# Attention parts dealt by their columns over one unit less, and a job's values one item later

## The chip, the core and the metric

The kernel runs on one core of a Trainium2 chip. The metric is the device time of one execution in microseconds. Three runs of the kernel before took 695.48, 698.78 and 702.34 us; the median is 698.78.

## The reference

Attention over 2 batches, 8 heads, 576 positions and heads of 64, with a bias from a running sum, feeds a two-layer block with an exponential unit, and that feeds four experts whose outputs are added with weights by token.

```python
scores = scale * np.matmul(q, k.transpose(0, 1, 3, 2))
cum = np.cumsum(np.maximum(s, 0.0), axis=-1)
bias = -(cum[:, :, :, None] - cum[:, :, None, :])
scores = np.where(causal, -1e9, scores + np.minimum(bias, 0.0))
attn = np.exp(scores - np.max(scores, axis=-1, keepdims=True))
attn = attn / (np.sum(attn, axis=-1, keepdims=True) + 1e-09)
x = np.matmul(attn, v)                        # then as 1152 rows of 512
h = x @ w_in                                  # 512 -> 2048
x = np.where(h > 0, h, np.exp(np.minimum(h, 0)) - 1) @ w_out
p = domain_probs / (domain_probs.sum(-1, keepdims=True) + 1e-09)
for e in range(4):                            # 512 -> 1024 -> 512
    out += p[:, e:e + 1] * (np.maximum(x @ w1[e], 0.0) @ w2[e])
```

## The kernel before

The 1152 tokens are worked in groups (`GROUPS`): a first group of 256 tokens, and the other 896 as two halves of 448 (`N2`). The attention of the first group is written out by hand at the start (`attention_first`). Then the first group goes through the first layer (`layer1`, 16 units of 128 hidden columns) and the experts (32 units), and the attention of all later tokens is threaded between these matmuls. Last, both layers are done for the 896 tokens (`both`), with the products of a Strassen scheme; this end is outside the change.

One unit is one call of `slot`: the up matmuls of a unit (12 of 256 columns in the experts, tile `up`), its activation (ScalarE and VectorE, tile `gt`), the preparation of a later unit's weights (ScalarE rounds them, VectorE takes the rest, tile `wu`), and the down matmuls of the unit some places back (6 of 512 columns, tiles `acc`). Units are numbered from 0; 16 is the end of the first layer, and 50 the end of the first group. Three times in a unit, at a third, at two thirds and at its end, `slot` calls `background`, and that hands out waiting work.

The waiting work is first the list of `attention_parts`. A job is one pair of heads of one batch and a range of queries (`JOBS`): 4 small jobs of 128 queries, then 4 of 320 and 4 of 448. Its items are blocks of 128 queries of one head (or 64 of both). Each item gives score parts (`scores`: matmuls L554, L556, L562, L563, on VectorE the bias and the maximum at L596, on ScalarE the exponential at L603), and three items later (`LATE`) transpose parts (`transposes`: VectorE's scaling L576 by `normalise`, TensorE L613, ScalarE's copy L625 or L628 into tile `pt`). After the transposes of a job's last item come its values (`values`: TensorE L640 reads `pt` and `v`; ScalarE copies the result into tile `xa` at L643), and behind them the loads of the job after next on SyncE's queue. The first score part of an item also prepares q and k of the next one where a new head begins (`split`: L539 to L542 on ScalarE, L90 on VectorE, two small loads at L536). Scores, transposes and values take their PSUM bank in turn from four (`ps_att`).

`Background` deals the list by count: at unit position `at` it has done the share of its parts that a line through (14, 0), (18, 0.06) and (45, 1) gives (`BG_FROM`, `BG_EVEN`, `BG_SLOW`, `BG_TO`). After 45 a second list is dealt out until 50 (`early_parts`): the splits of the later tokens' first blocks (tile `x2a`) and the sums and splits of the first two weight pairs of the end (tiles `sums`, `top`, `w`).

This order is what is written down; a scheduler then orders each engine's instructions by what it takes to be ready, so matmuls of one part can stand among those of another.

Of the kernel before, what the change touches and what calls it, by code (L numbers as in the profile page):

```python
# [37 lines left out]
LAG = 2  # L38
LATE = 3

BG_FROM, BG_EVEN, BG_TO = 14, 18, 45
BG_SLOW = 0.06

DEC = 4
# [8 lines left out]
def tile_kernel(ctx, tc, qT, kT, v, s, w64, w, probs, out):  # L53
# [20 lines left out]
    def sb(shape, tag, bufs, dtype=F32):  # L74
        p = (base if tag in BASE else edge if tag in EDGE else l1_pool if tag in L1
             else held if tag == "wr"
             else att_pool[0])
        return p.tile(shape, dtype, tag=tag, name=tag, bufs=bufs)
# [6 lines left out]
    def ps_att():  # L85
        n_att[0] += 1
        return ps(*(("att", 2), *spare)[n_att[0] % (1 + len(spare))])
# [363 lines left out]
    def attention_parts(x):  # L451


        items, jobs, small = [], [], []
        for b, chunks, col in JOBS:
            cb = CHUNKS[b]
            q0, q1 = cb[chunks[0]], cb[chunks[-1] + 1]
            for hp in range(HP):
                job = dict(b=b, chunks=chunks, col=col, q0=q0, q1=q1, hp=hp)
# [109 lines left out]
        def normalise(every=False):  # L569
            if not norm or len(norm) < 2 and not every:  # L570
                return
            sm = totals.pop()[:, :len(norm)]
            DVE.tensor_scalar(sm, sm, 1e-9, None, op0=ALU.add)
            DVE.reciprocal(sm, sm)
            for i, p in enumerate(norm):
                DVE.tensor_scalar(p, p, sm[:, i:i + 1], None, op0=ALU.mult)  # L576
            norm.clear()
# [28 lines left out]
        def transposes(it, cs):  # L606
            job, i, j, p = it["job"], it["i"], it["j"], it["p"]
            cb = CHUNKS[job["b"]]
            qo = cb[i] - job["q0"]
            normalise(it is items[-1])  # L610
            pt = ps_att().rearrange("p (c q) -> p c q", q=128)
            for m, c in enumerate(cs):
                PE.transpose(pt[:cb[c + 1] - cb[c], m, :], p[:, cb[c]:cb[c + 1]], ident)  # L613
            if "pt" not in job:
                job["pt"] = sb([128, 2, job["chunks"][-1] + 1, job["q1"] - job["q0"]], "pt", 2)
            dst, m0 = job["pt"], 0
            while m0 < len(cs):
                n = cb[cs[m0] + 1] - cb[cs[m0]]
                m1 = m0 + 1
                while m1 < len(cs) and cb[cs[m1] + 1] - cb[cs[m1]] == n:  # L620
                    m1 += 1
                c0, c1 = cs[m0], cs[m1 - 1] + 1
                if j is None:
                    for jj in range(2):
                        ACT.activation(dst[:n, jj, c0:c1, qo:qo + 64],  # L625
                                       pt[:n, m0:m1, 64 * jj:64 * jj + 64], AF.Copy)
                else:
                    ACT.activation(dst[:n, j, c0:c1, qo:qo + 128], pt[:n, m0:m1], AF.Copy)  # L628
                m0 = m1

        def values(job):
            cb = CHUNKS[job["b"]]
            hp, nq, n_c = job["hp"], job["q1"] - job["q0"], job["chunks"][-1] + 1
            normalise()
            o = ps_att()
            for c in range(n_c):
                n = cb[c + 1] - cb[c]
                qs = max(0, cb[c] - job["q0"])
                for j in range(2):
                    PE.matmul(o[64 * j:64 * j + 64, qs:nq], job["v"][:n, c, 64 * j:64 * j + 64],  # L640
                              job["pt"][:n, j, c, qs:nq], start=c == 0, stop=c == n_c - 1)
            xs = slice(job["col"], job["col"] + nq)
            ACT.activation(x[:, hp, xs], o[:, :nq], AF.Copy)  # L643
            if job in jobs and jobs.index(job) + 2 < len(jobs):
                load(jobs[jobs.index(job) + 2])

        def late():
            return tc.issue_after(last_coded[0].ins)

        def start():  # L650
            if small:
                with late():
                    load_small()
                split(items[0])
                split(items[1])
            with late():
                for job in jobs[:2]:
                    load(job)
            split(items[0])

        parts = [start, lambda: None]
        for n in range(len(items) + LATE):
            if n < len(items):
                it = items[n]
                w_ = CHUNKS[it["job"]["b"]][it["i"] + 1]
                cuts = [0, w_] if w_ <= 512 else [0, CUT, w_]
                cuts = [(a, e, a == 0, e == w_) for a, e in zip(cuts, cuts[1:])]
                for c in cuts:
                    def f(n=n, it=it, c=c):
                        if c[2] and n + 1 < len(items):  # L670
                            split(items[n + 1])
                        scores(it, c)
                    parts.append(f)
            if 0 <= n - LATE < len(items):
                it = items[n - LATE]
                cs = list(range(it["i"] + 1))
                for c in range(0, len(cs), 4):
                    parts.append(lambda it=it, cs=cs[c:c + 4]: transposes(it, cs))
                if it.get("last"):
                    parts.append(lambda job=it["job"]: values(job))  # L680
        return parts


    def three(o, a, b, first, last):
# [25 lines left out]

    class Background:
        def __init__(self, parts, points):
            self.parts, self.done, self.points = parts, 0, points

        def __call__(self, at):

            f = 0.0
            for (a, x), (b, y) in zip(self.points, self.points[1:]):
                f += (y - x) * min(max((at - a) / (b - a), 0.0), 1.0)
            while self.done < min(len(self.parts), f * len(self.parts)):  # L720
                self.parts[self.done]()
                self.done += 1

# [171 lines left out]
    def pair_steps(q):  # L895

        st = {}

        def sums():
            x = raws[q]  # L900
            st["t"] = t = a_tile([128, 4, 256], "sums", 1)
            b11, b12, b21, b22 = x[:, 0, 0:256], x[:, 1, 0:256], x[:, 0, 256:512], x[:, 1, 256:512]
            DVE.tensor_tensor(out=t[:, 0], in0=b12, in1=b11, op=ALU.subtract)
            DVE.tensor_tensor(out=t[:, 1], in0=b22, in1=b12, op=ALU.subtract)
            DVE.tensor_tensor(out=t[:, 2], in0=b22, in1=t[:, 0], op=ALU.subtract)
            DVE.tensor_tensor(out=t[:, 3], in0=b21, in1=t[:, 2], op=ALU.subtract)

        def high():
            tops[q] = a_tile([128, 2, 7, 256], "top", 2, F32R)
            w2s[q] = a_tile([128, 2, 2, 512], "w2", 2, F32R)  # L910
            x, o = raws[q], tops[q]
            ACT.activation(o[:, 0, 0:2].rearrange("p a b -> p (a b)"), x[:, 0, 0:512], AF.Copy)  # L912
            ACT.activation(o[:, 0, 2], x[:, 1, 256:512], AF.Copy)

        def low():
            x, o = raws[q], tops[q]
            split_lo(o[:, 1, 0:2].rearrange("p a b -> p (a b)"), x[:, 0, 0:512],
                     o[:, 0, 0:2].rearrange("p a b -> p (a b)"))
            split_lo(o[:, 1, 2], x[:, 1, 256:512], o[:, 0, 2])

        def high_t():
            ACT.activation(tops[q][:, 0, 3:7], st["t"], AF.Copy)

        def low_t():
            split_lo(tops[q][:, 1, 3:7], st["t"], tops[q][:, 0, 3:7])

        def high_2():
            ACT.activation(w2s[q][:, 0], raws[q][:, :, 512:1024], AF.Copy)

        def low_2():  # L930
            split_lo(w2s[q][:, 1], raws[q][:, :, 512:1024], w2s[q][:, 0])
            if q + N_WR < n_pair:
                load_pair(q + N_WR)

        return [high, low, sums, high_t, low_t, high_2, low_2]
# [3 lines left out]
    def first_blocks(x):  # L939

        xa = a_tile([128, 2, NCC, N2], "x2a", 1, F32R)
        fs = []
        for i, name in ((0, "A11"), (2, "A12")):
            def f(i=i, name=name):
                blocks[name] = xa[:, :, i:i + 2]
                ACT.activation(xa[:, 0, i:i + 2], x[:, i:i + 2, 0:N2], AF.Copy)
                split_lo(xa[:, 1, i:i + 2], x[:, i:i + 2, 0:N2], xa[:, 0, i:i + 2])
            fs.append(f)
        return fs

    def early_parts(x):

        pools["a"] = ctx.enter_context(tc.tile_pool(name="l2a", bufs=1, reuse_waits="tile"))
        return first_blocks(x) + pair_steps(0) + pair_steps(1)

    for m in range(E * NCD + LAG):
        slot(NAB + m, NAB + LAG + m, up2(NAB + m, m) if m < E * NCD else None, background)
# [165 lines left out]
    parts = {}  # L1123
# [48 lines left out]
```

## Time and profile before

| | |
|---|---|
| median of three runs | 698.78 us |
| the profiled execution | 697.03 us |
| its span, first to last instruction | 695.3 us |
| TensorE, matmuls busy | 684.2 us (98%), 3544 records |
| TensorE, weight loads busy | 584.3 us (84%) |
| VectorE busy | 584.2 us (84%) |
| ScalarE busy | 374.2 us (54%) |
| later attention in the trace | 66.9 to 235.5 us |

Matmuls overlap, so the busy time of TensorE (PE) hides short stops. Its weight loads (PEld) stop as soon as the next matmul's data is missing. DVE is VectorE, ACT is ScalarE, SPq is the queue of SyncE that issues transfers. Lines are those of the kernel before.

### The profile page before, as it was taken

To read this page: it belongs to the slowest core of one execution; us is meant where nothing else is said; L and a number is where in the kernel's file an instruction comes from. 1 tells how busy PE (TensorE), PEld (TensorE's weight loads), DVE (VectorE), ACT (ScalarE), POOL (GpSimd) and SP (SyncE) were. 2 spreads that over 40 slices of the span, in tenths; PEclk is the share of its full clock that TensorE was granted. 3 is DMA by queue.
4 is the path that set the end of the run, shared out by engine and by line. 5 is a ranking of instruction groups with operands and counts; after the bars stand their busy time and mean duration, and the time that the engine had idled before them with its cause. 6 is when DMAs were issued, how large, how long until landed. Compare 5 with 4: busy or idle time off the path is not lost.

```text
span 695.3 us, 9816 instructions
## 1 busy us (share of the span) xinstructions
PE 684.2 (98%) x3544; PEld 584.3 (84%) x3544; DVE 584.2 (84%) x1138; ACT 374.2 (54%) x766; POOL 14.3 (2%) x34
## 2 busy tenths in 40 slices
PE   9999999999999999999999999999999999999997
PEld 7788787768877788999999878888888888888886
DVE  7999698878877799889999999988888888888765
ACT  6998798778786757555555542333332222223220
POOL 5011000000000000000000000000000000000000
PEclk9999999999999999999999999999999999999999
DMA  8999965555432140111111111011111111110002
GB/s 295 407 364 383 264 196 181 158 149 150 150 111 91 30 152 1 60 61 61 60 62 62 60 61 45 22 58 59 60 62 60 62 61 60 62 61 0 1 0 107
DMA packets 30831, 75.63 MB, mean 109 GB/s; under 512 B 3904, under 2 KB 12224, under 8 KB 30784
## 3 DMA queue, kind: packets, MB, share of 16 engines
q1 hardware_dynamic: 29104, 69.42, 30.3%
q0 software_dynamic: 1536, 5.46, 2.0%
q8 instruction: 28, 0.46, 0.3%
q14 instruction: 19, 0.16, 0.1%
q10 hardware_dynamic: 144, 0.13, 0.1%
HBM read 67.18 MB, written 7.82 MB: 108 GB/s over the span
## 4 chain that ended last, share of the span: by engine, by line
PE 79%; ACT 8%; DVE 7%; DMA 4%; issue 2%; SPq 1%; DVEq 0%; ACTq 0%
PE acc L687 37%; PE att L976 15%; PE up L976 11%; PE up L687 5%; PE acc L640 2%; DMA pt<-in_kT 2%; PE att L640 2%; DMA yl<-in_w 2%; ACT p L603 1%; ACT z L170 1%; DVE S L90 1%; PE att L613 1%; PE acc L613 1%; ACT wu L113 1%; DVE p L596 1%
## 5 line engine op out<-in xcount | busy, mean ns | idle before, releaser
L687 PE MATMUL acc<-w,h 128*128 128x512 f32 x672 | 171.0, 392 | 0.0
L687 PEld LDWEIGHTS acc<-w,h 128*128 128x128 f32 x672 | 126.1, 188 | 21.9 <-ACT h L995 0.2
L976 PE MATMUL att<-S,top 128*128 128x448 f32 x432 | 99.6, 365 | 1.0 <-DVE u L1002 0.7
L749 DVE SCALAR_TENSOR_TENSOR xa<-acc,pr,xa 128x512 f32<-128x512 f32 x105 | 78.5, 747 | 16.6 <-PE acc L687 15.3
L976 PEld LDWEIGHTS att<-S,top 128*128 128x128 f32 x432 | 80.7, 188 | 11.3 <-DVE u L1002 1.5
L687 PE MATMUL acc<-h,w 128*128 128x448 f32 x384 | 86.6, 365 | 0.3 <-DVE h L90 0.3
L995 ACT ACTIVATE h<-c 128x448 fp32r<-128x448 f32 x48 | 27.4, 574 | 110.2 <-DVE c L1002 110.2
L687 PEld LDWEIGHTS acc<-h,w 128*128 128x128 f32 x384 | 71.2, 188 | 8.0 <-DVE h L90 0.7
L976 PE MATMUL up<-x2a,top 128*128 128x448 f32 x288 | 66.0, 366 | 0.1
L976 PEld LDWEIGHTS up<-x2a,top 128*128 128x128 f32 x288 | 53.9, 188 | 6.7 <-ACT top L912 0.5
L687 PE MATMUL acc<-wu,gt 128*128 128x512 f32 x192 | 56.7, 407 | 0.0
L687 PE MATMUL up<-yh,wu 128*128 128x256 f32 x256 | 53.1, 288 | 0.0
L1002 DVE TENSOR_TENSOR c<-att,u 128x448 f32<-128x448 f32 x70 | 43.6, 624 | 9.8 <-PE att L976 8.9
L996 DVE SCALAR_TENSOR_TENSOR h<-c,h 128x448 fp32r<-128x448 f32 x48 | 29.8, 623 | 18.8 <-ACT h L995 18.8
L687 PEld LDWEIGHTS up<-yh,wu 128*128 128x128 f32 x256 | 42.1, 190 | 1.9 <-issue 0.9
L90 DVE TENSOR_TENSOR wu<-raw,wu 128x1024 fp32r<-128x1024 f32 (+1 forms) x33 | 39.2, 1190 | 5.3 <-ACT wu L113 5.3
L995 ACT ACTIVATE h<-up 128x448 fp32r<-128x448 f32 x16 | 8.7, 543 | 58.7 <-PE up L976 58.7
L687 PEld LDWEIGHTS acc<-wu,gt 128*128 128x128 f32 x192 | 33.8, 189 | 6.4 <-issue 1.8
L1087 DVE TENSOR_TENSOR ox<-acc,ox 128x448 f32<-128x448 f32 x56 | 34.3, 619 | 4.5 <-PE acc L687 4.3
L603 ACT ACTIVATE p<-p,nm 128x384 f32<-128x384 f32 (+4 forms) x56 | 34.5, 616 | 4.7 <-DVE nm L596 4.4
L687 PE MATMUL up<-yl,wu 128*128 128x256 f32 x128 | 36.5, 285 | 0.1
L976 PE MATMUL up<-S,top 128*128 128x448 f32 x144 | 34.4, 366 | 1.0 <-ACT S L1057 0.5
(211 smaller groups left out, 1220.5 us busy)
## 6 DMA issues: line engine op xcount, KB each, us to landing
raw<-in_w SPq DMA_DIRECT2D x35, 512.0 KB
wr<-in_w SPq DMA_DIRECT2D x16, 1024.0 KB
wu<-in_w SPq DMA_DIRECT2D x10, 512.0 KB
w_dec<-wu POOLq DMA_DIRECT2D x10, 512.0 KB, 8.9
wr<-w_dec SPq DMA_DIRECT2D x5, 1024.0 KB
k<-in_kT SPq DMA_DIRECT2D x16, 288.0 KB
cd<-in_w SPq DMA_DIRECT2D x6, 512.0 KB
xa<-in_w SPq DMA_DIRECT2D x6, 512.0 KB
```

Source lines behind the costliest of these rows:

```text
L90: return DVE.tensor_tensor(out=lo, in0=x, in1=hi.bitcast(F32), op=ALU.subtract)
L113: ACT.activation(t[:, 0, r], x[:, r], AF.Copy)
L603: ACT.activation(p, p, AF.Exp, bias=nm, scale=-1.0, accum_out=sm)
L613: PE.transpose(pt[:cb[c + 1] - cb[c], m, :], p[:, cb[c]:cb[c + 1]], ident)
L640: PE.matmul(o[64 * j:64 * j + 64, qs:nq], job["v"][:n, c, 64 * j:64 * j + 64], job["pt"][:n, j, c, qs:nq], start=c == 0, stop=c == n_c - 1)
L687: PE.matmul(o, a[m], b[n], start=first and i == 0, stop=last and i == 2)
L749: DVE.scalar_tensor_tensor(out=o_sb, in0=o, scalar=pr[:, i, e:e + 1], in1=o_sb, op0=ALU.mult, op1=ALU.add)
L976: PE.matmul(bank, tops[q][:, m, op, cs], x[:, n, c], start=first and c + i == 0, stop=c == 1 and i == 2, skip_group_check=True)
L995: ACT.activation(h[:, 0, u, cs], c, AF.Relu)
L996: DVE.scalar_tensor_tensor(out=h[:, 1, u, cs], in0=c, scalar=0.0, in1=h[:, 0, u, cs].bitcast(F32), op0=ALU.max, op1=ALU.subtract)
L1002: DVE.tensor_tensor(out=t, in0=a, in1=b, op=ALU.add)
L1087: DVE.tensor_tensor(out=y[:, c, cs], in0=o, in1=y[:, c, cs], op=ALU.add)
```

## The change

The parts now carry a weight each: a score part 0.2 + 1.2 per thousand columns, and 1.0 more where a new head's split hangs on it; a transpose part 0.2 + 0.7 per thousand columns; values and the start 0.5. `Background` hands out by the sum of weights in place of the count, and an empty part after the start is gone. `BG_TO` goes from 45 to 44: the later attention is dealt over one unit less, and the second list starts one unit sooner (its parts all weigh 1.0). And a job's values no longer stand right behind its last transposes: they are kept in `ready` and written down after the scores of the next item. What is computed stays the same.

```diff
--- before.py
+++ after.py
@@ -38,7 +38,7 @@
 LAG = 2
 LATE = 3
 
-BG_FROM, BG_EVEN, BG_TO = 14, 18, 45
+BG_FROM, BG_EVEN, BG_TO = 14, 18, 44
 BG_SLOW = 0.06
 
 DEC = 4
@@ -647,6 +647,9 @@
         def late():
             return tc.issue_after(last_coded[0].ins)
 
+        def work(columns, each):
+            return 0.2 + each * columns / 1000
+
         def start():
             if small:
                 with late():
@@ -658,7 +661,7 @@
                     load(job)
             split(items[0])
 
-        parts = [start, lambda: None]
+        parts, ready = [(0.5, start)], []
         for n in range(len(items) + LATE):
             if n < len(items):
                 it = items[n]
@@ -670,15 +673,20 @@
                         if c[2] and n + 1 < len(items):
                             split(items[n + 1])
                         scores(it, c)
-                    parts.append(f)
+                    after = items[n + 1] if n + 1 < len(items) else it
+                    head = after["job"] is not it["job"] or after["j"] != it["j"]
+                    parts.append((work(c[1] - c[0], 1.2) + (1.0 if c[2] and head else 0.0), f))
+            if ready:
+                parts.append(ready.pop())
             if 0 <= n - LATE < len(items):
                 it = items[n - LATE]
                 cs = list(range(it["i"] + 1))
                 for c in range(0, len(cs), 4):
-                    parts.append(lambda it=it, cs=cs[c:c + 4]: transposes(it, cs))
+                    parts.append((work(128 * len(cs[c:c + 4]), 0.7),
+                                  lambda it=it, cs=cs[c:c + 4]: transposes(it, cs)))
                 if it.get("last"):
-                    parts.append(lambda job=it["job"]: values(job))
-        return parts
+                    ready.append((0.5, lambda job=it["job"]: values(job)))
+        return parts + ready
 
 
     def three(o, a, b, first, last):
@@ -710,14 +718,15 @@
 
     class Background:
         def __init__(self, parts, points):
-            self.parts, self.done, self.points = parts, 0, points
+            self.parts, self.done, self.points = [f for _, f in parts], 0, points
+            self.upto = [sum(w for w, _ in parts[:i]) for i in range(len(parts) + 1)]
 
         def __call__(self, at):
 
             f = 0.0
             for (a, x), (b, y) in zip(self.points, self.points[1:]):
                 f += (y - x) * min(max((at - a) / (b - a), 0.0), 1.0)
-            while self.done < min(len(self.parts), f * len(self.parts)):
+            while self.done < len(self.parts) and self.upto[self.done] < f * self.upto[-1]:
                 self.parts[self.done]()
                 self.done += 1
 
@@ -951,7 +960,7 @@
     def early_parts(x):
 
         pools["a"] = ctx.enter_context(tc.tile_pool(name="l2a", bufs=1, reuse_waits="tile"))
-        return first_blocks(x) + pair_steps(0) + pair_steps(1)
+        return [(1.0, f) for f in first_blocks(x) + pair_steps(0) + pair_steps(1)]
 
     for m in range(E * NCD + LAG):
         slot(NAB + m, NAB + LAG + m, up2(NAB + m, m) if m < E * NCD else None, background)
```

The order of TensorE at three places, before and after. In the names, `ident,p` are transposes, `pt,v` values, `kh,qs` and `kl,qb` scores, `wu,gt` down matmuls and `wu` with `yh` or `yl` up matmuls of an expert; in the first layer both read `wu`, with `gt` and `xf`. Lines after the change are 9 higher from the expert matmuls on.

The values of the third job of 320 queries, before:

```order
L613 MATMUL acc_1749<-ident,p 128x128 x4
L640 MATMUL att<-pt,v 64x320
L687 MATMUL acc_1700<-wu,gt 128x512 x3
L640 MATMUL att<-pt,v 64x320 x5
L640 MATMUL att<-pt,v 64x192 x2
L640 MATMUL att<-pt,v 64x64 x2
L554 MATMUL acc_1783<-kh,qs 128x384
L556 MATMUL acc_1783<-kl,qb 128x384
```

The same job's values, after:

```order
L613 MATMUL acc_1757<-ident,p 128x128 x4
L695 MATMUL acc_1678<-wu,gt 128x512 x3
L554 MATMUL att<-kh,qs 128x384
L556 MATMUL att<-kl,qb 128x384
L640 MATMUL acc_1774<-pt,v 64x320
L695 MATMUL up<-yh,wu 128x256
L640 MATMUL acc_1774<-pt,v 64x320 x5
L640 MATMUL acc_1774<-pt,v 64x192 x2
L640 MATMUL acc_1774<-pt,v 64x64 x2
```

The down matmuls and the next score pair moved from behind the first values to ahead of them. ScalarE at the same place, before (L628 is the copy that these values read, L643 takes them out):

```order
L628 ACTIVATE pt<-acc_1749 128x4x128
L542 ACTIVATE qb<-q_1767 64x448
L643 ACTIVATE xa<-att 128x320
L628 ACTIVATE pt<-att 128x3x128
L603 ACTIVATE p,sm<-p,nm 128x384
```

ScalarE there, after:

```order
L628 ACTIVATE pt<-acc_1757 128x4x128
L542 ACTIVATE qb<-q_1786 64x448
L603 ACTIVATE p,sm<-p,nm 128x384
L113 ACTIVATE wu<-raw 128x1024
L643 ACTIVATE xa<-acc_1774 128x320
L879 ACTIVATE gt<-up 128x256
L628 ACTIVATE pt<-att 128x3x128
```

An exponential and a weight copy now stand ahead of L643. TensorE at the last values of the later attention, before:

```order
L640 MATMUL acc_2882<-pt,v 64x448 x3
L640 MATMUL acc_2882<-pt,v 64x320 x2
L640 MATMUL acc_2882<-pt,v 64x192 x2
L640 MATMUL acc_2882<-pt,v 64x64 x2
L687 MATMUL up<-yh,wu 128x256
L687 MATMUL up<-yl,wu 128x256
L687 MATMUL up<-yh,wu 128x256 x2
L687 MATMUL up<-yl,wu 128x256
L687 MATMUL up<-yh,wu 128x256
L687 MATMUL acc_2863<-wu,gt 128x512 x3
```

The last values, after:

```order
L695 MATMUL acc_2893<-wu,gt 128x512
L640 MATMUL acc_2853<-pt,v 64x448 x3
L640 MATMUL acc_2853<-pt,v 64x320 x2
L640 MATMUL acc_2853<-pt,v 64x192 x2
L640 MATMUL acc_2853<-pt,v 64x64 x2
L695 MATMUL acc_2893<-wu,gt 128x512 x2
L695 MATMUL acc_2894<-wu,gt 128x512 x3
```

`acc_2863` before and `acc_2893` after are the same expert's sums: the values moved from the middle of the next unit's up matmuls to behind the first down matmul of the unit ahead of it.

## Rows read from the trace of the kernel before

**Rows 1.** The page: span, and TensorE's busy time and instructions.

```profile
span 695.3 us, 9816 instructions
PE 684.2 (98%) x3544; PEld 584.3 (84%) x3544; DVE 584.2 (84%) x1138; ACT 374.2 (54%) x766; POOL 14.3 (2%) x34
```

**Rows 2.** Stretch; length, PE, PEld, DVE, ACT, POOL busy (count); granted clock; DMA share; GB/s.

```profile
66.90:235.50 168.60, 165.67 (x1053) 132.99 (x1052) 132.53 (x358) 134.19 (x326) 0.53 (x1) 1.00 0.54 158
235.50:245.40 9.90, 9.90 (x68) 9.12 (x67) 9.71 (x16) 7.73 (x13) 0.00 (x0) 1.00 0.05 7
245.40:270.00 24.60, 23.43 (x110) 19.67 (x109) 23.91 (x37) 14.54 (x24) 0.00 (x0) 1.00 0.28 105
```

**Rows 3.** Chain that ended last, 235 to 250 us: start, length, what.

```profile
235.66 1.43 PE up L687 x12
237.10 1.39 PE acc L687 x6
```

**Rows 4.** Waits of the weight loads, 66.9 to 235.5: total us, times, longest.

```profile
PEld acc L640 <- issue: 3.1, 13, 0.3
PEld att L640 <- ACT pt L628: 2.7, 5, 1.0
PEld att L640 <- issue: 2.3, 9, 0.4
...
PEld acc L640 <- ACT pt L628: 1.5, 4, 0.7
PEld acc L613 <- DVE p L576: 1.2, 2, 0.7
...
PEld acc L562 <- ACT pt L625: 0.6, 1, 0.6
```

**Rows 5.** Timeline at one job's values: start, length, instruction, idle before and releaser.

```profile
138.74 0.60 PE L613 MATMUL acc<-ident,p 128*128 128x128 f32 x4
...
139.27 0.75 PE L640 MATMUL att<-pt,v 128*64 128x320 f32 x2
...
139.95 0.96 PE L687 MATMUL acc<-wu,gt 128*128 128x512 f32 x3
...
140.85 0.58 ACT L628 ACTIVATE pt<-acc 128x512 f32<-128x512 f32 x1
...
141.48 1.81 PEld L640 LDWEIGHTS att<-pt,v 128*64 128x64 f32 x14 [1.00 <-ACT pt L628]
```

**Rows 6.** Waits of ScalarE, 66.9 to 235.5 us.

```profile
ACT xa L643 <- PE acc L640: 9.0, 4, 2.9
ACT xa L643 <- PE att L640: 7.7, 4, 2.2
```

**Rows 7.** Waits of SyncE's queue, 66.9 to 235.5 us (L505 loads v).

```profile
SPq L505 <- PE att L640: 9.0, 4, 4.0
```

**Rows 8.** Timeline at the first later score.

```profile
70.73 0.19 PEld L554 LDWEIGHTS att<-kh,qs 128*128 128x128 f32 x1 [0.66 <-ACT kh L540]
```

**Rows 9.** Timeline at the last values.

```profile
230.52 2.84 PE L640 MATMUL acc<-pt,v 128*64 128x448 f32 x18
...
231.42 0.42 DVE L906 TENSOR_TENSOR sums<-wr,sums 128x256 f32<-128x256 f32 x1
...
234.83 1.09 DVE L90 TENSOR_TENSOR x2a<-xa,x2a 128x896 fp32r<-128x896 f32 x1 [2.99 <-ACT x2a L946]
```

**Rows 10.** Groups by line, whole span: count | busy us, mean ns | idle before.

```profile
L777 PE MATMUL acc<-gt,wu 128*128 128x256 f32 x80 | 19.4, 382 | 0.0
```

**Rows 11.** Groups by line of VectorE, 235.5 to 270 us.

```profile
L90 DVE TENSOR_TENSOR wu<-raw,wu 128x1024 fp32r<-128x1024 f32 x2 | 2.4, 1222 | 0.2 <-ACT wu L113 0.2
```

**Rows 12.** Waits of the weight loads, 245.4 to 270 us.

```profile
PEld att L976 <- DVE u L1002: 0.7, 1, 0.7
PEld acc L687 <- DVE h L90: 0.7, 1, 0.7
PEld acc L976 <- DVE A L90: 0.6, 1, 0.6
```

## The prediction

> **What bounds the kernel now.** I read the page first: TensorE is busy for 684.2 of 695.3 us [rows 1]. Busy time here is the union of overlapping matmuls, so it hides short stalls; the next view was therefore the busy time by stretch [rows 2]. Later attention is threaded through the matmuls of the first token group from 66.9 to 235.5 us. There the weight loads (PEld) fill 132.99 of 168.6 us, VectorE 132.53 and ScalarE 134.19, about 79% each: none of them is full, and TensorE goes from one job to the next with small holes. Behind it, from 235.5 to 245.4, TensorE runs without attention, and the chain shows its undisturbed pace: 12 matmuls of 256 columns in 1.43 us (0.119 each), 6 of 512 columns in 1.39 us (0.231 each) [rows 3]. From 245.4 to 270 VectorE is full (23.91 of 24.6 us) and TensorE waits for it; after that the program is the same before and after and stalls little. So only holes in 66.9 to 270 us can be won or lost. The change neither adds nor removes a matmul, a copy or a transfer: both orders have 3288 matmuls and equal kinds.
>
> **Part 1: values follow one item later.** The waits of the weight loads [rows 4] name the holes at the values: 2.7 + 1.5 = 4.2 us in 9 stops for the copy of the transposed probabilities (ScalarE, L628). The timeline of one such job [rows 5] shows how: the last transposes run at 138.74, one pair of value matmuls at 139.27, three down matmuls, and then TensorE has nothing left in its order: the copy starts at 140.85, and the values only at 141.48. In the new order three down matmuls and a whole score pair (0.69 + 0.35 us) stand between these transposes and the first values, and a single pair, then one more matmul, precedes the rest. For the other large jobs I count in the new order between 0.8 us (the last job) and over 3 us of matmuls at that place. A stop of this kind cannot go to zero: even where nothing is waited for, PEld idles 3.1 + 2.3 = 5.4 us in 22 stops at the value matmuls ("issue" in [rows 4]), 0.25 us each. So 4.2 - 9 x 0.25 = 2.0 us can be won and 0 must be. I take 1.6, because ScalarE also changes: before, the copy that takes the values out (L643) stood next in its order and it idled for 9.0 + 7.7 = 16.7 us in 8 jobs [rows 6]; now an exponential and a weight copy stand ahead of it, so that time does work and the next copies come sooner.
>
> The values are also less cut up. In the order before, the 12 jobs' values stand in 20 separate pieces, now in 14. At 0.25 us a piece, 6 x 0.25 = 1.5 us at most; part of that idle lies under the matmul still running, so the bounds are 0 and 1.5, and I take 1.0.
>
> What is late next: the values carry the loads of the job after next (one q, two k, two v issues on SyncE). SyncE waits there for the values already [rows 7], and behind it stand the row loads that the scores need. Counting matmuls at the two paces above, the scores that read those rows come at least 6.8 us after the releasing values before and at least 8.0 us now, so I cost this at 0. Without that cover a late row load would stop the scores, and then the transposes behind them.
>
> **Part 2: the handing-out by columns.** The 142 parts were dealt by count over units 14 to 45, now 141 by weight over 14 to 44. From the code, a unit's load (in the new weights) ran from 1.9 to 5.0 between units 18 and 44; now from 2.1 to 4.9 between 18 and 43. Most units lie nearer the mean, the extremes do not. The holes it can touch are the transposes that wait for VectorE's scaling and the scores that wait for a bank: 1.2 + 0.6 = 1.8 us [rows 4]. As many new ones can appear, since the new order was made afresh: bounds -1.8 and +1.8. I take -0.6, a third, as ScalarE is freer.
>
> The first scores move ahead of two down matmuls of the first layer. They already wait 0.66 us of PEld time for the split that hangs on a transfer, and that transfer does not move. The two matmuls that stood ahead of it take 19.4 / 80 = 0.24 us each [rows 8, 10], so up to 0.5 us more is lost there, or nothing if the transfer lands sooner than in this execution. I take +0.4.
>
> **Part 3: one unit less.** The last values end earlier against the end of the group: counting in the orders, 43 up and 42 down matmuls follow them before, 48 and 47 now, so 5 x 0.119 + 5 x 0.231 = 1.75 us more room. That room matters because VectorE idled there: 2.99 us, from the last of the sums to the first split of the new blocks [rows 9], and was then full to 270 us. Against it, VectorE now has one more weight split (1.22 us, [rows 11]) behind the last values. Net 0.5 us less backlog at the hand-over, where PEld waits 0.7 + 0.7 + 0.6 = 2.0 us for VectorE [rows 12]. Bounds 0 and -2.0; I take -0.5.
>
> **Sum.** -1.6 - 1.0 - 0.6 + 0.4 - 0.5 = -3.3 us. The profiled execution took 697.03 us (span 695.3 and 1.7 around it), which gives 693.7; the median shown is 698.78, 1.75 above it, so the forecast for the median is 695.5. The bounds together: best -2.0 - 1.5 - 1.8 + 0 - 2.0 = -7.3, worst 0 + 0 + 1.8 + 0.5 + 0 = +2.3, or 691.5 to 701.1.
>
> **The rivals.** *The waits only move* (698.8): the program is ordered anew, and each stop removed at a value is answered by one at a transpose or a score. For it: VectorE and ScalarE are at 79% and any order leaves some. Against it: the 16.7 us that ScalarE stood still at the values is the largest wait of the stretch, and it is what changes. *All holes close* (691.5): the best bounds above. For it: all four terms lean on one cause, ScalarE late behind the values. Against it: three of the eight large jobs still have only 0.8 to 1.05 us of cover, and VectorE remains full to 270 us.
>
> *Slower, at the copy of the values*: ScalarE stands 2.1 us per large job before L643 (16.7 / 8, [rows 6]). If, with the values later, the transposed copy that TensorE needs next stands right behind L643, TensorE loses what a group of 12 up matmuls (1.43 us) doesn't cover, 0.7 us a job, 5.6 in eight; less the 1.0 of the pieces that is +4.6, or 703.4. It decides from the point where ScalarE idles more than 1.4 us before L643 and a copy L628 comes next. The order shows L628 soon behind in several jobs; against it, the exponential and the weight copy now ahead of L643 shorten the wait itself. [...]
>
> *The stretch becomes as dense as the one without attention*: PEld fills 9.12 of 9.9 us there, 92%, against 79% [rows 2]; closing that would give 0.13 x 168.6 = 22 us, or 677. [...] Against it as a size: attention's matmuls are of other shapes, the value matmuls load 64 columns for a row of 320, and the named stops of [rows 4] add up to a third of the 22.
>
> **How the numbers follow.** The forecast (a saving of 1.5 to 5.5 us): 0.56. Waits only move: 0.22. All holes close: 0.11. Slower at the copy: 0.09. As dense as without attention: 0.02. The predicted time is the first's, 695.5. The range 691 to 701 takes in the bounds and leaves out the last case, half of the slower one and a little of the best: under 0.2. A measurement of this kernel tells about 1%, 7 us, from no change. Faster by more than that needs the best bounds or beyond: 0.09. Slower by more needs more than the slower rival's price: 0.03. Within 1%: 0.88.
>
> **What would show it.** Right: PEld's waits at the values for L628 fall from 4.2 us to about 2, its "issue" stops there from 22 to about 16, ScalarE's idle before L643 falls well under 16.7 us, the last values, which end at 233.4 us before (230.52 + 2.84, [rows 9]), end several us sooner, and the waits after 245 shrink a little. The clock is granted in full (1.00) in every stretch before [rows 2], and should stay so. Wrong: new stops of a microsecond at the transposes or scores, SyncE holding back a weight load so that ScalarE waits for a transfer, or a stretch 245 to 270 that is no shorter. What would upset it most is a stop that all the later units inherit, such as a row load landing after its scores are due.

## The result, and the profile after

The changed kernel takes 690.25 us (median of four runs, 688.72 to 691.47), beside 698.35 for the kernel before (four runs). The ratio is 0.9886, 95% interval 0.9845 to 0.9928. It is faster by 1.1%, and just outside the range given (691.0 to 701.0). Measured again beside 17 runs of the kernel before it stood at 689.78 against 697.04, ratio 0.9894 (0.9849 to 0.9938). About one execution in eight of the kernel before takes 6 to 7 us longer than the rest, and its medians of three and four runs (698.78, 698.35) stand 1.3 to 2.4 us above those of 17 to 32 runs (696.3 to 697.0).

The page of the changed kernel; against [rows 1] the span is 6.3 us shorter:

```profile
span 689.0 us, 9834 instructions
PE 679.1 (99%) x3544; PEld 582.8 (85%) x3544; DVE 584.8 (85%) x1138; ACT 375.1 (54%) x766; POOL 14.3 (2%) x34
```

Busy time by stretch, columns as in [rows 2], each bound but the first moved by the 6.2 us that are gone by then:

```profile
66.90:229.30 162.40, 161.55 (x1058) 132.90 (x1057) 135.35 (x364) 136.02 (x329) 0.88 (x2) 1.00 0.56 165
229.30:239.20 9.90, 9.90 (x68) 9.13 (x67) 9.90 (x16) 6.88 (x11) 0.00 (x0) 1.00 0.32 106
239.20:263.80 24.60, 23.43 (x110) 19.66 (x109) 22.89 (x35) 14.53 (x24) 0.00 (x0) 1.00 0.18 65
```

The weight loads do the same work in the first stretch (132.90 against 132.99 us) in 6.2 us less; the other two stretches are as long as before, down to 23.43 us of TensorE in 24.6. The whole gain lies inside the threaded attention.

A measure that leaves the start of the program out is the **stretch**: from the first later score to the first matmul of the last part (tile `up<-x2a`). It begins at the same time as before [rows 8]. The timelines of the kernel before (its end) and of the changed one (both ends):

```profile
249.50 1.77 PE L976 MATMUL up<-x2a,top 128*128 128x448 f32 x8
```

```profile
70.74 0.19 PEld L554 LDWEIGHTS att<-kh,qs 128*128 128x128 f32 x1 [0.68 <-ACT kh L540]
...
243.27 5.02 PE L985 MATMUL up<-x2a,top 128*128 128x448 f32 x24
```

It is 249.50 - 70.73 = 178.8 us before and 243.27 - 70.74 = 172.5 after: 6.2 us less (172.6 in the second profile of the changed kernel). In every profile here, what follows it, to the end of the span, takes 445.4 to 447.0 us.

The waits of the weight loads in the first stretch, to be set beside [rows 4]:

```profile
PEld acc L640 <- issue: 3.7, 15, 0.3
PEld att L640 <- issue: 1.8, 7, 0.3
...
PEld acc L640 <- ACT pt L628: 0.8, 3, 0.4
...
PEld att L640 <- ACT pt L628: 0.7, 3, 0.2
```

The waits for the copy L628 fell from 4.2 to 1.5 us. The stops called issue did not fall: 22 before, 22 now, 5.4 and 5.5 us. ScalarE's idle before it takes the values out (L643), to be set beside the 16.7 us of [rows 6], is 5.1:

```profile
ACT xa L643 <- PE acc L640: 3.8, 3, 2.6
...
ACT xa L643 <- PE att L640: 1.3, 2, 0.8
```

And the hand-over to the last part, beside [rows 12], has not changed at all:

```profile
PEld att L985 <- DVE u L1011: 0.7, 1, 0.7
PEld acc L695 <- DVE h L90: 0.7, 1, 0.7
PEld acc L985 <- DVE A L90: 0.6, 1, 0.6
```

By the two views of the stretch above, TensorE's busy time fell from 165.67 to 161.55 us, by 4.1, and its idle time (the length less the busy time) from 2.93 to 0.85 us, by 2.1. So two thirds of the 6.2 us came out of busy time, for which no list of waits has a line. The 2.7 us of PEld's waits can't be added to it: PEld can wait while a matmul still runs, as in [rows 5], where its 1.00 us before 141.48 begin at 140.48 and the down matmuls run to 140.91. Most of the busy time was lost on the value matmuls. Busy time of TensorE on L640 alone, before and after (columns: stretch, length, PE, PEld, clock, DMA share, GB/s):

```profile
66.90:245.40 178.50, 29.35 (x176) 13.10 (x176) 1.00 0.51 150
```

```profile
66.90:245.40 178.50, 25.61 (x176) 12.44 (x176) 1.00 0.55 164
```

The same 176 records take 3.7 us less. The timeline tells why. Before, in six of the eight large jobs the first value matmul stood alone: 0.75 us for its two records at 139.27, other matmuls, then 18 more records [rows 5]. In a seventh it ran alone ahead of a stop (20 records in 3.61 us at 192.40). After, two jobs are still cut like that, and six run in one piece. One of each in the changed kernel, with the matmuls that follow (L695 is L687 before):

```profile
139.11 0.75 PE L640 MATMUL acc<-pt,v 128*64 128x320 f32 x2
139.79 0.38 PE L695 MATMUL up<-yh,wu 128*128 128x256 f32 x1
140.15 2.42 PE L640 MATMUL acc<-pt,v 128*64 128x320 f32 x18
142.49 0.39 PE L695 MATMUL up<-yl,wu 128*128 128x256 f32 x1
...
191.71 2.85 PE L640 MATMUL att<-pt,v 128*64 128x448 f32 x20
194.49 0.44 PE L613 MATMUL acc<-ident,p 128*128 128x128 f32 x2
```

A job's values belong to two heads, and a record of either is listed with `128*64`, where a down matmul has `128*128`. In one piece the two heads' records start together: the first two at 191.71 begin 0.01 us apart. Counted to the start of the next matmul, 20 records take 2.35 us at 320 queries and 2.78 at 448; 18 records take 2.35 and 2.77, no less, since one of the heads still has all its ten records to do; and the lone matmul comes on top, 0.68 us at 320 queries and 0.89 or 0.90 at 448. Call this theory A: what the later place cures is that one head runs ahead of the other. Its rivals: P, only the wait at the copy counts; B, the dealing by columns and the shorter stretch do the work.

### The profile page after: what moved, and what is told of

The parts are those of the page before. It is cut to its first block, busy times and chain, and to the rows that moved or that the text cites. A ratio compares the mean times of both kernels' runs of the same rounds, so it can differ in the third digit from the quotient of the medians.

```text
span 689.0 us, 9834 instructions
## 1 busy us (share of the span) xinstructions
PE 679.1 (99%) x3544; PEld 582.8 (85%) x3544; DVE 584.8 (85%) x1138; ACT 375.1 (54%) x766; POOL 14.3 (2%) x34
## 4 chain that ended last, share of the span: by engine, by line
PE 83%; DMA 7%; DVE 5%; ACT 5%; issue 1%; SPq 0%; DVEq 0%; ACTq 0%
PE acc L695 39%; PE att L985 15%; PE up L985 11%; PE up L695 6%; DMA pt<-in_kT 2%; PE acc L640 2%; DMA yh<-in_w 2%; PE att L613 1%; PE acc L613 1%; PE att L640 1%; DMA v<-in_v 1%; ACT z L170 1%; DVE S L90 1%; DMA q<-in_qT 1%; ACT wr L160 1%
## 5 line engine op out<-in xcount | busy, mean ns | idle before, releaser
L695 PE MATMUL acc<-w,h 128*128 128x512 f32 x672 | 171.1, 392 | 0.0
L695 PEld LDWEIGHTS acc<-w,h 128*128 128x128 f32 x672 | 126.1, 188 | 21.9 <-ACT h L1004 0.2
L695 PE MATMUL acc<-h,w 128*128 128x448 f32 x384 | 86.6, 365 | 0.3 <-DVE h L90 0.3
L695 PEld LDWEIGHTS acc<-h,w 128*128 128x128 f32 x384 | 71.2, 188 | 8.1 <-DVE h L90 0.7
L695 PE MATMUL acc<-wu,gt 128*128 128x512 f32 x192 | 55.7, 404 | 0.0
L695 PE MATMUL up<-yh,wu 128*128 128x256 f32 x256 | 53.3, 288 | 0.0
L695 PEld LDWEIGHTS up<-yh,wu 128*128 128x128 f32 x256 | 42.0, 190 | 2.5 <-issue 1.4
L695 PEld LDWEIGHTS acc<-wu,gt 128*128 128x128 f32 x192 | 34.0, 189 | 4.8
L113 ACT ACTIVATE wu<-raw 128x1024 fp32r<-128x1024 f32 (+1 forms) x33 | 33.8, 1027 | 5.2 <-PE acc L695 3.3
L695 PE MATMUL up<-yl,wu 128*128 128x256 f32 x128 | 36.5, 285 | 0.0
```

Of the source, the lines that this page charges most:

```text
L113: ACT.activation(t[:, 0, r], x[:, r], AF.Copy)
L695: PE.matmul(o, a[m], b[n], start=first and i == 0, stop=last and i == 2)
```

## Experiments

Each run is an edit of the kernel before or of the changed kernel, as the columns of the table say; "heads together" is an edit of this study. Times are medians, in brackets the median of the kernel before measured beside it; the stretch is of the profiled execution; the last column is TensorE's busy time on the value matmuls.

| values | dealt by | to unit | heads | time, us | stretch | values |
|---|---|---|---|---|---|---|
| old place | count | 45 | free | 696.3 to 697.0 (before) | 178.8 | 29.35 |
| old place | columns | 45 | free | 700.94 (696.34) | 183.1 | 31.37 |
| old place | count | 44 | free | 697.42 (696.71) | 178.7 | 27.97 |
| old place | columns | 44 | free | 699.71 (696.71) | 181.9 | 30.79 |
| later | count | 45 | free | 692.82 (696.71) | 174.7 | 25.72 |
| later | columns | 45 | free | 692.69 (696.34) | 174.8 | 26.57 |
| later | count | 44 | free | 690.44 (696.34) | 172.3 | 24.61 |
| later | columns | 44 | free | 689.78 (697.04) (after) | 172.5 | 25.61 |
| old place | count | 45 | together | 691.78 (696.71) | 174.7 | 22.85 |
| old place | columns | 45 | together | 695.29 (696.88) | 176.5 | 22.84 |
| later | count | 45 | together | 692.07 (697.04) | 173.1 | 22.84 |
| later | count | 44 | together | 689.34 (696.88) | 172.2 | 22.84 |
| later | columns | 44 | together | 687.72 (696.34), 688.67 (697.04) | 170.7 | 22.85 |
| later | columns | 43 | together | 692.23 (696.88) | 173.9 | 22.84 |
| later | columns | 44 | one after the other | 710.35 (696.88) | 191.9 | 43.16 |

**The three parts of the change, each alone and in pairs.** Values later alone (the last of the edited lines; `ready` is filled and emptied as in the change):

```diff
-                    parts.append(lambda job=it["job"]: values(job))
+                    ready.append(lambda job=it["job"]: values(job))
```

> Only the values go one item later; the parts are dealt by count over the old 31 units. Theory A (the lone pair: when the two heads' value matmuls are issued apart, the first pair runs alone and costs 0.68 us at 320 columns, 0.89 at 448, as 139.27 to 139.95 in the trace of before): six such splits of before fall to one, 0.89 left of 4.5, so -3.6 us, and what else the later place saves in waits at the copy (4.2 us before, about 1.5 left in the changed kernel), together -5 to -7. Theory B (the dealing by columns and the shorter stretch do the work, the values only follow): -2.6 us at most, the prediction's own terms for this part. Theory C (all three parts are needed together): less than half of the change's -8.

Ratio 0.9938 (0.9915 to 0.9961), the stretch 4.1 us shorter: more than the prediction's terms for this part (2.6), less than theory A's 5 to 7, and by the medians (-3.9 of -8) just under half of the change, theory C's mark, though by the stretch it is two thirds. Besides the one split left, two jobs run with a lone matmul and a stop inside one piece (20 records in 3.46 and 3.52 us), which the order alone had not shown.

The changed kernel with the values at the old place:

```diff
-                    ready.append((0.5, lambda job=it["job"]: values(job)))
+                    parts.append((0.5, lambda job=it["job"]: values(job)))
```

> The changed kernel with the values at their old place: dealing by columns and one unit less stay. Theory A (lone pairs): the order has two splits at 320 columns and four at 448, 2 x 0.68 + 4 x 0.89 = 4.9 us against 4.5 before, so +0.4 and the waits at the copy as before: -1 to +1.5 us against before. Theory B (dealing and shorter stretch do the work): -4 to -7 us. Theory C (all needed together): -1 to -4.

Ratio 1.0043 (1.0014 to 1.0072): slower than before, and 3.1 us more of stretch. Theories B and C fall, both of which forecast a gain, and the loss is larger than theory A's count.

The unit alone (`BG_TO` 44 in the kernel before):

> Only the end of the stretch moves from unit 45 to 44; dealing by count, values at the old place. The order made afresh has two splits at 320 columns and none at 448 (before four and two). Theory A (lone pairs): 1.36 against 4.5 us, so about -3 us although neither the values' place nor the dealing changed. Theory P (it is the postponement and the wait at the copy): -0.5 to 0. Theory B (a shorter stretch gains at the hand-over to the last part): -1 to -2, seen behind 245 us.

Ratio 1.0001 (0.9965 to 1.0037), stretch the same to 0.1 us. That is the number of theory P. Theory A as I had written it missed: it counted splits in the order. On the chip three of the "whole" jobs run the lone matmul first too, and then stand still for the copy. Timeline of this run, matmuls, at the first job of 320 queries:

```profile
105.78 0.75 PE L640 MATMUL att<-pt,v 128*64 128x320 f32 x2
106.86 2.42 PE L640 MATMUL att<-pt,v 128*64 128x320 f32 x18 [0.33 <-ACT pt L628]
```

Nothing is put in between any more, so the stop costs at least what the split cost (3.42 us from 105.78 to the next matmul at 109.20, against 2.35 in one piece). What counts is whether the second head's copy has landed when the values come up (PEld waits 0.89 us for it before 106.86), not how the order is cut.

The dealing by columns alone (the diff of the change without `ready` and with `BG_TO` 45), and then the changed kernel with `BG_TO` 45:

> Only the dealing by columns (and the dropped empty part); values at the old place, the stretch to unit 45 as before. Theory A (lone pairs): four splits at 320 and four at 448 columns, 6.3 us against 4.5 before, and eight lone small ones: +1.5 to +3 us, slower than before. Theory B (dealing by columns is the gain): -2 us or more. The prediction's term for this part: -0.6.

> The changed kernel with the stretch to unit 45 as before: dealing by columns and values later. Theory A (lone pairs): one split at 448 left, 0.89 against 1.57 us in the changed kernel: as fast as the changed one, within 1 us of it (-7 to -9 against before). Theory B (the shorter stretch matters): 1 to 2 us slower than the changed kernel (-6 to -7).

The first: ratio 1.0076 (1.0048 to 1.0103), 4.3 us more of stretch, all eight large jobs split. The second: 0.994 (0.9928 to 0.9953), as fast as values later alone (174.8 and 174.7). It is 2.2 us of stretch longer than the changed kernel; theory A had it as fast, counting one split, but three of its large jobs begin with a lone matmul, and theory B's 1 to 2 us comes nearer. With the values later, the dealing by columns is worth nothing (0.1 and 0.2 us of stretch to unit 45 and 44); with the values at the old place it costs 3 to 4 us.

Values later and unit 44, dealt by count:

```diff
-BG_FROM, BG_EVEN, BG_TO = 14, 18, 45
+BG_FROM, BG_EVEN, BG_TO = 14, 18, 44
```

> Values later and the stretch to unit 44, dealing by count. Theory A (lone pairs): no split left: 1.6 us less than the changed kernel by this alone, if the dealing by columns is worth nothing: -8 to -10 against before. Theory B (dealing by columns matters): 2 us or more slower than the changed kernel, -4 to -6.

Ratio 0.9921 (0.9894 to 0.9947), stretch 172.3, 0.2 us from the changed kernel: the same gain without the dealing by columns, so theory B falls. Theory A's 1.6 us more did not come; one job still runs its first matmul alone ahead of a stop (20 records in 3.67 us). So of the 6.2 us, 4.1 come with the later values, 2.4 with unit 44 on top of them, and the dealing takes 0.2 back. Theory C falls with that: two of the three parts give all of it.

**The two heads.** To test theory A by itself, the values were kept in place and only bound together: the head whose copy comes last is written first, and the other is queued behind its first matmul.

```diff
-            o = ps_att()
+            o, lead = ps_att(), None
...
-                for j in range(2):
-                    PE.matmul(o[64 * j:64 * j + 64, qs:nq], ...
+                for j in (1, 0):
+                    with tc.issue_after(lead.ins) if lead and j == 0 else nullcontext():
+                        mm = PE.matmul(o[64 * j:64 * j + 64, qs:nq], ...
+                    lead = lead or mm
```

In the kernel before:

> The kernel before, with one change in the values: the head whose copy comes last is issued first and the other head's matmuls are kept behind its first one, so that the two heads always run side by side and no pair runs alone (12 pieces instead of 20, no split). Theory A (lone pairs): 4.5 us of pairs that ran alone are gone; where the copy is late the lone pair had filled the wait, so up to 0.7 us comes back in each of the jobs that wait (five at the first loads): -1 to -4.5 us. Theory P (the wait at the copy is all that counts, the lone pair lies in it): 0, within 1 us.

Ratio 0.9918 (0.9889 to 0.9946), stretch 4.1 us shorter. The value matmuls take 22.85 us of TensorE instead of 29.35, though the waits of PEld for L628 are still 3.9 us, against 4.2. Timeline of the job of [rows 5] in this run:

```profile
139.79 2.42 PE L641 MATMUL att<-pt,v 128*64 128x320 f32 x20 [0.86 <-ACT pt L628]
142.14 0.55 PE L613 MATMUL att<-ident,p 128*128 128x128 f32 x3
```

It waits 0.86 us and then does everything in 2.35. The busy time of the whole stretch, the kernel before and then this run (columns as in [rows 2]):

```profile
70.73:249.50 178.77, 176.10 (x1120) 142.68 (x1121) 143.38 (x369) 140.28 (x335) 0.00 (x0) 1.00 0.50 147
```

```profile
69.19:243.93 174.74, 170.03 (x1123) 140.47 (x1122) 143.62 (x370) 139.97 (x335) 0.00 (x0) 1.00 0.52 153
```

TensorE is busy for 6.1 us less and idle for 2.0 us more: the lone matmuls had filled waits for a third of their time, and the rest was lost. Theory P, which has them lie wholly in such waits and forecast no change, falls as the only cause.

In the changed kernel, twice:

> The changed kernel, with the other head's value matmuls kept behind the first of the head whose copy comes last: no split. Theory A (lone pairs): the two splits left (0.68 + 0.89) are gone: -1 to -1.6 us against the changed kernel, -9 to -10 against before. Theory P (the wait at the copy is all): no change against the changed kernel, -8.

> The changed kernel with heads kept together, again, now in the same call as the changed kernel. Theory A (two heads' matmuls apart in two jobs still): 1.5 to 2.5 us below the changed kernel. Theory P (only the wait at the copy counts): no difference.

Ratios 0.9875 (0.9861 to 0.9888) and 0.9862 (0.9826 to 0.9898); the second is 1.1 us below the changed kernel measured beside it, and there is 1.9 us less of stretch in both profiles (170.7 twice). By the medians this difference is within their scatter. The stretch has it in both profiles of this one order, and it is near the price of the two lone matmuls that were left (0.68 + 0.89 us). This is the fastest version of the study.

The opposite, the two heads one behind the other (the loops change places, and all matmuls of the second head are queued behind the last of the first):

```diff
-            for c in range(n_c):
...
+            for j in (1, 0):
+                for c in range(n_c):
...
```

> The changed kernel with the two heads of every job issued one behind the other: all value matmuls of the one head, then all of the other; nothing else. Theory A (side by side two heads take the time of one; alone each takes its own 0.27 us per pass of 320 columns as at 139.27 to 139.95 in the trace of before): the value time doubles, from 25 us to 41 to 47, and the kernel gets 13 to 20 us slower than the changed one. Rival (the lone matmul is dear only because it stands between matmuls of other shapes, a price of each switch): no switch more than in the changed kernel, within 2 us of it.

Ratio to the kernel before 1.0193 (1.0151 to 1.0234); against the changed kernel it is 20 us slower, and 19.4 us longer in its stretch, and the value matmuls take 43.16 us, as theory A has it (41 to 47). The rival of a price at each switch of shape (within 2 us) falls. Timeline of a job of each size:

```profile
111.88 4.75 PE L641 MATMUL acc<-pt,v 128*64 128x320 f32 x20
116.56 0.55 PE L613 MATMUL att<-ident,p 128*128 128x128 f32 x3
...
183.47 5.60 PE L641 MATMUL acc<-pt,v 128*64 128x448 f32 x20
189.01 0.44 PE L613 MATMUL att<-ident,p 128*128 128x128 f32 x2
```

Counted to the next matmul the 20 records take 4.68 and 5.54 us, twice the 2.35 and 2.78 (1.99). So side by side the two heads take half the time that they take in turn. The 0.27 us of the expectation is what a head's records of 320 columns take inside a piece (in the kernel before they start at 141.80, 142.07 and 142.34); the two of 139.27 to 139.95 take 0.34 each.

The dealing by columns with heads together:

> The run with the dealing by columns alone (values at the old place, stretch to unit 45, 4.6 us slower than before by the medians) with the two heads' value matmuls kept together: no matmul of one head runs alone ahead of the other. Theory A (what the dealing alone lost, it lost at heads that ran apart: 6.3 us in eight large jobs): -5 to -7 us against that run, so 0 to -2 against before. Theory W (it lost them in waits at the copy, since the values come sooner behind their transposes): the waits stay or grow by what the lone matmul had filled: -2 us or less against that run, +2 to +5 against before.

695.29, ratio 0.9984 (0.9959 to 1.0009), and 6.6 us less of stretch than the same kernel with its heads free. So of the 4.3 us that the dealing by columns lost alone, 2.5 are the heads running apart, as theory A has it. It is still 1.8 us longer than the kernel before with heads together, and here theory W has a part: the waits of its values for L628 are 6.4 us against 3.9. Kernel before with heads together, then this one:

```profile
PEld att L641 <- ACT pt L628: 2.4, 4, 1.2
...
PEld acc L641 <- ACT pt L628: 1.5, 3, 1.1
```

```profile
PEld att L641 <- ACT pt L628: 3.4, 5, 1.2
PEld acc L641 <- ACT pt L628: 3.0, 6, 0.9
```

Both edits on the kernel before, values later and heads together:

> Kernel before with two edits: values one item later, and the two heads kept together; dealing by count, stretch to unit 45. Its neighbours: only heads together 691.8 (-4.9), only values later 692.8 (-3.9). If heads running apart is all that the postponement cures: 691.8, within 1 us, like heads together alone. If the postponement also takes the wait at the copy away: 2 us or more below that, 688 to 690.

692.07, ratio 0.9926 (0.9894 to 0.9957). The median says no difference to heads together alone (691.78); the stretch is 1.6 us shorter (173.1 against 174.7). The waits of PEld for L628 at its values are down from 3.9 to 2.2 us, by about as much:

```profile
PEld acc L641 <- ACT pt L628: 1.1, 1, 1.1
...
PEld att L641 <- ACT pt L628: 1.1, 1, 1.1
```

So each edit alone gives 4.1 us of stretch and both give 5.7: of the postponement's 4.1, about 2.5 go with the heads, and 1.6 remain with the heads together. That these 1.6 are the wait is not shown: TensorE's idle time in the stretch fell by 0.8 us only (4.7 to 3.9). The medians of these runs can't separate 1.6 us, the split rests on one profile each, and it is no more than what a new order alone moves below.

**The unit and the dealing, with heads together.**

> The changed kernel with heads kept together (687.7 us) and the stretch to unit 43. If a shorter stretch gives by itself (as 45 to 44 gave 2.2 us with the values later): 1 to 3 us less, 685 to 687. If 44 only fell well by the order made afresh: 687.7, within 2 us either way.

> Values later, stretch to unit 44, heads kept together, parts dealt by count. If the dealing by columns is worth nothing once the values come later (as the two runs with it and without it say, 0.2 us apart): 687.7 like the changed kernel with heads kept together, within 1 us. If it gains: 1.5 us or more slower than that, 689 or more.

Unit 43 is 3.2 us of stretch longer than 44 (692.23 us), which neither expectation had. So a shorter stretch does not gain by itself; what in the order makes 43 longer is not shown. Dealing by count is 1.5 us longer than by columns (689.34), at the edge that the expectation set; beside 1.8 the other way at unit 45 and the old place, and 0.1 and 0.2 with the heads free, this reads as the scatter of orders made afresh, and not as a gain of the dealing.

Keeping the heads together shortens the stretch in all five surroundings that the table has with and without it, by 4.1, 6.6, 1.6, 0.1 and 1.8 us. The 0.1 stands where the values come later by count to unit 44: there the value matmuls had only 1.8 us left to lose, and TensorE's idle time grew by 1.1 us (1.5 to 2.7).

**The size.**

> The changed kernel itself, unedited, beside the same runs of the kernel before. In the first measurement before stood at 698.35 (four runs), in all later ones at 696.3 to 696.9. If those four were high: 690.3, 6 to 6.5 us below before (ratio 0.991). If the change is worth the full 8.1 us: 688.5, ratio 0.9886.

689.78 against 697.04, 7.3 us by the medians, ratio 0.9894 (0.9849 to 0.9938), and 172.6 us of stretch. The stretch says 6.2; where the 1.1 us lie that the medians add to it is not shown.

## Why the prediction was right and wrong

It had the direction, the place (only 66.9 to 245 us) and one of the two causes (values standing too close behind their copy), and missed the size: a saving of 3.3 us forecast, 6.2 in the profiled executions and 7 to 8 in the medians. The step that failed is the price of a piece in part 1: the cost of cutting a job's values was taken for a short stop, and it is a matmul of one head that runs without the other's.

- **The waits at the values**, -1.6 with a bound of -2.0: the named waits fell by 2.7 us. The bound was wrong. I had kept 0.25 us for each of nine entries, taken from the stops called issue, and forecast 22 of these to become 16. They stayed 22. All 22 of the changed kernel lie inside a run of values, between its records (17 of the 22 before), so they set no floor for a wait at its entry. One of them, in the split job above, before the last four records:

```profile
142.23 0.19 PEld L640 LDWEIGHTS acc<-pt,v 64*64 64x64 f32 x4 [0.28 <-issue]
```

- **Fewer pieces**, -1.0 at 0.25 us a piece, bound -1.5: this is the term that was mis-sized most. The value matmuls take 3.7 us less of TensorE. A piece was priced by its stop, while the price is the matmul that runs without its partner, 0.68 or 0.90 us; seven large jobs paid it before and two after. The rows were at hand: 0.75 us for 2 records in [rows 5] against 2.84 for 18 in [rows 9], 0.38 and 0.16 us a record. Heads together in the kernel before (-4.1 us of stretch with the values left at their place) and the heads one after the other (+19.4 us) show the price. Nor do the pieces of the order count it: to unit 44 alone, three jobs that are whole in the order paid it too.
- **The dealing by columns**, -0.6: 0.1 to 0.2 us the other way with the values later, 4.3 (to unit 45) and 3.2 us (to 44) slower with the values at the old place. The bound of ±1.8 had no room for that: it counted only waits at transposes and scores, while the new order to unit 45 split all eight large jobs.
- **The first scores**, +0.4: nothing. They wait 0.68 us, against 0.66 [rows 8]. That this term and the one before came out near 0 is luck for the sum: their errors nearly cancel.
- **One unit less**, -0.5 at the hand-over: nothing there, the three waits are the same to 0.1 us. To unit 44 the stretch is 2.2 to 2.4 us shorter once the values come later, 0.9 by count with heads together as well, and 0.1 in the kernel before. So this term is too small by some 2 us and its reason, the room at the hand-over, is not the one; what the order to 44 gains stays open.
- **The row loads behind the later loads**, costed at 0: right. SyncE waits at L505 for the values for 6.6 + 3.9 us now, against 9.0 [rows 7], and no score stops for a row.
- **The base.** The forecast was tied to a median of 698.78, some 2 us above what many runs of the kernel before give. Against 696.7 its 695.5 is a saving of 1.2 us only.

Of its signs, the waits for L628, ScalarE's idle time and the last values (they end at 222.42 + 2.84 = 225.3 us, not 233.4) came as said; the stops called issue and the waits behind 245 us did not.

Of the rivals, the slower one fell: ScalarE idles 5.1 us before L643 and not 16.7, 0.6 a large job, under its mark of 1.4, though one wait of 2.6 is above it. "All holes close" (691.5) came nearest in time, for a wrong reason: most stops of PEld stayed, and two thirds of the gain came out of the busy time, which none of the cases counted. That TensorE could get as dense as without attention did not come: PEld fills 132.90 of 162.4 us, 82%.

## What to carry to other kernels

Price a split run by the duration of its first piece and of the rest, not by the idle time beside it: busy time can be as wasteful as a stop (here 0.68 us for a lone matmul at 320 queries), and the lists of waits have no line for a head that runs without the other. Where two chains can run side by side on TensorE, as the two heads do here (2.35 us, against 4.68 in turn), write first the one whose input lands last and queue the other behind it, so that the scheduler can't send one ahead (here 4.9 us in the kernel before). And where an edit makes a scheduler order everything anew, expect a scatter in either direction beside the effect that was meant, here of 1.5 to 3.2 us; only crossed runs separate the two.

## What the hardware showed that was not expected

TensorE does not always go through the start of the program at the same pace, and the granted clock listed does not show it. The same eight matmuls (L319) run several times there. The first time they take 1.65 us in the kernel before and in the second profile of the changed kernel alike. The timeline of both at the first and the second time, the kernel before first:

```profile
4.77 1.65 PE L319 MATMUL acc<-pt 64*128 64x128 f32 x8
...
7.54 0.93 PE L319 MATMUL acc<-pt 64*128 64x128 f32 x8
```

```profile
4.77 1.65 PE L319 MATMUL acc<-pt 64*128 64x128 f32 x8
...
8.35 1.65 PE L319 MATMUL acc<-pt 64*128 64x128 f32 x8
```

So the kernel before has come to a quicker pace by then, and the other profile has not. The busy time of its first stretch (columns as in [rows 2]), and before it that of the kernel before:

```profile
5.40:20.00 14.60, 14.43 (x114) 10.32 (x114) 13.28 (x64) 12.16 (x45) 4.56 (x8) 1.00 0.96 358
```

```profile
5.40:27.00 21.60, 21.60 (x112) 16.45 (x112) 14.74 (x66) 12.43 (x44) 4.49 (x8) 1.00 1.00 383
```

114 matmuls are done in 14.6 us there, and here 112 take 21.6; the first score stands at 76.7 us instead of 70.7, with the same stretch behind it. The listed granted clock is 1.00 in both, so it does not show what slows TensorE; no run here tells the cause.
